# Attention scores in a ring of half banks, the softmax bias on VectorE, and other durations for the planner

## The chip, the cores and the metric

The kernel runs on one core of a Trainium2 chip. TensorE (PE) multiplies, VectorE (DVE) and ScalarE (ACT) work element by element and can read and write PSUM, GpSimd (POOL) works on SBUF, and SyncE (SP) issues most of the transfers. Each engine takes its instructions in the order in which they were written for it, and waits where an instruction names a semaphore that has not been reached. The metric is the device time of one launch in microseconds (us); the reference point is the median of three runs.

## The reference

Two independent halves are computed and put side by side in the output (2048 rows, 1024 + 1024 columns):

- A, attention over a sliding window: `qkv = x @ wqkv`, 32 heads of 32 columns, scores `q k^T / sqrt(32)` where `0 <= i - j < 256`, softmax, times `v`, then `@ wo`.
- B, a Fourier mixing layer by matrices: `a = x @ Wd_re^T`, `b = x @ Wd_im^T`, `y = Ws_re @ a - Ws_im @ b`.

All inputs and outputs are float32.

## The kernel before

Every large product is done on float16 pieces: a float32 operand is scaled and split into a high and a low float16 part, and three of the four part products are summed in PSUM (line 720). Blocks of such products are further combined by a scheme with seven instead of eight block products, whose sums and differences are made by POOL and DVE. A product tile is 128 partitions by 512 columns, one PSUM bank of 2 KB per partition, and it is filled by groups of matmuls; ACT and DVE then move it out.

Attention is done in 256 **blocks**: 8 groups of four heads, 16 tiles of 128 query rows, and two pairs of heads per group. The function `s_step` (line 562 on) records one block, for two heads j = 0, 1 at a time:

1. PE, line 586: scores of the query tile against its own and the previous key tile, 2 x 256 columns, into a tile `s`. For the tiles from the third on, a second product against the key tile two back, 2 x 128 columns, into a tile `old`. Together these are called score groups here: 256 into `s`, 224 into `old`.
2. DVE, line 597: a predicated copy that puts the entries of `old` that are inside the window over those of `s` that lie above the diagonal (or a constant where there is no `old`).
3. DVE, line 602: the negated maximum of each row, `mx`.
4. POOL, line 609: `bias = mx * scale + constant`, 128 x 2 values.
5. ACT, line 612: the exponential of each head's scores, in place in `s`, with that bias.
6. ACT, line 432, the high part, then DVE, line 436, the low part, both from `s` into the SBUF tile `hl`.
7. SP: a transposing transfer of `hl` into `t`; POOL, lines 627 and 630: masks on `t`; four blocks later PE, line 662: the product with `v` into the bank `pv`.

The eight PSUM banks are used thus: four for the products `m` (line 720), two for `s` (a ring of two tiles, each a whole bank for the two heads of a block), one for `old`, one for `pv`. `old` also takes the small transposes with which scale factors are found (lines 471 and 1058), read by DVE in lines 473 and 1060.

The order of all instructions is made by a list scheduler in the kernel's own Python (`Plan`). Every operation is recorded with an engine, an estimated duration, the buffers it reads and writes, and a ring: buffer k of a ring of n can be written when the last users of buffer k - n are done. PE operations get a due time from the sum of their durations, the others from what waits for them; each engine, when free, takes the ready operation that is due first. The operations are then issued in the order of their planned starts. What follows from that order is not the planner's: the framework that builds the program looks at the tiles that each instruction reads and writes, in that order, and adds the semaphore waits between engines. The planner knows only the buffers and keys that it was given.

Durations enter the plan as numbers: `c_act` for ACT, `c_mm` for matmuls, 0.26 for a small transpose, 0.034 for a matmul with `v`.

Of the kernel before, what the change touches and what calls it, by code (L numbers as in the profile page):

```python
# [10 lines left out]
F32 = mybir.dt.float32  # L11
# [6 lines left out]
ALU = mybir.AluOpType  # L18
AX = mybir.AxisListType

P = 128
# [28 lines left out]
BIAS = "POOL"  # L50
# [250 lines left out]
def c_act(n, ap=True):  # L301
    return 0.19 + 0.00084 * n + (0.09 if ap else 0.0)
# [26 lines left out]
def c_mm(n):  # L329
    return max(0.032, n / 2400.0 + 0.0025)  # L330
# [3 lines left out]
def fused_kernel(ctx: ExitStack, tc: tile.TileContext, xa, wqk, wv, wo, xb, wd, cs, out):  # L334
# [14 lines left out]
    ps_s = ctx.enter_context(tc.tile_pool(name="ps_s", bufs=2, space=PSUM))  # L349
# [17 lines left out]
    pshift = const.tile([P, 1], F32, name="pshift")  # L367
# [10 lines left out]
    def setup():  # L378
# [5 lines left out]
        nc.gpsimd.memset(pshift, PSHIFT)  # L384

    op("POOL", 1.0, setup, w=["ident", "upper", "never", "pshift"])
# [3 lines left out]
    old_ring = Ring(R, lambda k: ps_v.tile([P, CH], F32, tag="old", name=f"old_{k}"), 1, free=True)  # L390
    s_ring = Ring(R, lambda k: ps_s.tile([P, 2, 2 * P], F32, tag="s", name=f"s_{k}"), 2)
# [54 lines left out]
    def dve(cost, fn, r=(), w=(), port=False):  # L446
        op("DVE", cost, fn, r=r, w=w, port=port)
# [20 lines left out]
    def scale_of(key, v, s, wk, down=2.0 ** -14, loose=False):  # L468
        t1 = tops.pop(key)
        pt = old_ring.new()  # L470
        op("PE", 0.26, lambda: nc.tensor.transpose(pt.t[:, :P], t1.t[:, 0:1].to_broadcast([P, P]), ident),
# [8 lines left out]
        dve(0.53, rest, w=[wk])  # L480
# [48 lines left out]
    def attention():  # L529
# [33 lines left out]
        def s_step(b):  # L563
# [4 lines left out]
            S = s_ring.new()  # L568
# [3 lines left out]
            def scores(dst, k0, k_end, w):  # L572
                mats, cost, keys = [], 0.0, []
                for j in range(2):
                    h, k = 2 * hp + j, k0
                    while k < k_end:
# [4 lines left out]
                        cost += c_mm((k1 - k) * P) + 0.01  # L581
# [14 lines left out]
            sv = lambda: S.t[:, :, 2 * P - w:2 * P]  # L596
            dve(0.425, lambda: nc.vector.copy_predicated(  # L597
                S.t[:, :, P:2 * P], upper2,
                old.t[:, :2 * P].rearrange("p (j k) -> p j k", j=2) if nb == 3 else never2),
                r=["upper", "never"] + ([old] if nb == 3 else []), w=[(S, 0), (S, 1)])  # L600
            mx, bias = mx_ring.new(), bias_ring.new()
            dve(c_dve(2 * w), lambda: nc.vector.tensor_reduce(mx.t, sv(), axis=AX.X, op=ALU.max, negate=True),  # L602
                r=[(S, 0), (S, 1)], w=[mx])
            es = escs[:, g // 2, sc:sc + 1]
            if BIAS == "ACT":
                op("ACT", 0.387, lambda: nc.scalar.activation(bias.t, mx.t, AF.Identity, bias=pshift, scale=es),
                   r=[mx, "pshift", ("esc", g // 2)], w=[bias])
            else:
                op("POOL", 0.215, lambda: nc.gpsimd.tensor_scalar(bias.t, mx.t, es, PSHIFT, op0=ALU.mult, op1=ALU.add),  # L609
                   r=[mx, ("esc", g // 2)], w=[bias], port=True)  # L610
# [1084 lines left out]
```

## Time and profile before

| what | value |
|---|---|
| median of three runs | 1731.82 us (1731.67 to 1733.55) |
| profiled execution | 1732.34 us, its span 1730.6 us |
| PE busy | 1690.7 us (98% of the span), granted clock 1.00 |
| DVE busy | 1346.4 us (78%) |
| ACT busy | 1056.7 us (61%) |
| POOL busy | 776.7 us (45%) |

The span runs from the first to the last instruction, and the execution takes 1.7 us more than its span. Attention lies between the first score matmul at 262.4 us and the end of the last low part at 1504.1 us. A busy PE in these tables is PE with a matmul in flight. "Idle before" is time in which an engine had nothing running, with the instruction that ended it.

### The profile page before, as it was taken

How to read it: one execution, taken by the hardware profiler on the slowest of the kernel's cores; microseconds unless marked ns; L12 is line 12 of the kernel's file. 1: busy time of each engine (PE TensorE's matmuls, PEld its weight loads, DVE VectorE, ACT ScalarE, POOL GpSimd, SP SyncE). 2: the span in 40 equal slices, each digit the busy share in tenths (PEclk: the TensorE clock that was granted, in tenths of full speed). 3: DMA queues.
4: the chain of work that ended last, by engine and by line, in shares of the span. 5: the costliest groups of instructions: out<-in, count | busy, mean ns of one | idle time of the engine just before them, and what ended most of it. 6: DMA issues, size and time to landing. Idle time of an engine off the chain costs nothing.

```text
span 1730.6 us, 31866 instructions
## 1 busy us (share of the span) xinstructions
PE 1690.7 (98%) x11607; PEld 907.7 (52%) x11607; DVE 1346.4 (78%) x2294; ACT 1056.7 (61%) x1678; POOL 776.7 (45%) x979
## 2 busy tenths in 40 slices
PE   8999999999999999999999999999999999999998
PEld 3446787674545445545445555545555555544443
DVE  6978997677987888777798986789886688879641
ACT  7555635456767778777685756676665676553322
POOL 0133501314545646535765755676564666611000
PEclk9999999999999999999999999999999999999999
DMA  6389799999999779898499999769999658983331
GB/s 261 124 321 334 233 306 263 279 227 240 230 258 235 145 192 233 205 271 202 96 220 279 254 266 215 145 141 237 245 258 231 151 128 204 221 269 110 110 98 73
DMA packets 469918, 368.36 MB, mean 213 GB/s; under 512 B 341760, under 2 KB 412416, under 8 KB 469760
## 3 DMA queue, kind: packets, MB, share of 16 engines
q1 hardware_dynamic: 468896, 363.17, 81.0%
q0 software_dynamic: 864, 3.15, 1.2%
q8 instruction: 91, 1.49, 0.4%
q14 instruction: 67, 0.55, 0.1%
HBM read 195.97 MB, written 96.86 MB: 169 GB/s over the span
## 4 chain that ended last, share of the span: by engine, by line
PE 54%; DVE 15%; issue 8%; DMA 7%; ACT 7%; POOL 7%; SPq 1%; POOLq 0%; DVEq 0%; ACTq 0%
PE m L720 48%; PE pv L662 3%; POOL raw L1075 2%; DVE mx L602 2%; DVE st L1102 2%; ACT s L612 2%; POOL bias L609 2%; PE s L586 2%; DVE hl L436 2%; DMA t<-hl 1%; DVE s L597 1%; POOL t L630 1%; POOL z L627 1%; ACT hl L432 1%; DMA qk<-qs 1%
## 5 line engine op out<-in xcount | busy, mean ns | idle before, releaser
L720 PE MATMUL m<-reg,st 128*128 128x512 f16 x4776 | 1093.6, 379 | 13.6 <-DVE st L1102 3.6
L720 PEld LDWEIGHTS <-st 128*128 128x128 f16 x5400 | 512.5, 97 | 583.8 <-issue 15.1
L612 ACT ACTIVATE s<-s,bias,escs 128x256 f32<-128x256 f32 (+1 forms) x512 | 271.1, 530 | 286.2 <-POOL bias L609 277.4
L609 POOL TENSOR_SCALAR bias<-mx,escs 128x2 f32<-128x2 f32 x256 | 120.9, 472 | 400.5 <-DVE mx L602 308.6
L1075 POOL TENSOR_TENSOR raw<-raw,raw 128x512 f32<-128x512 f32 x128 | 175.8, 1374 | 186.6 <-DVE st L1102 174.7
L436 DVE TENSOR_TENSOR hl<-s,hl 128x512 f16<-128x512 f32 (+1 forms) x256 | 171.1, 669 | 96.5 <-ACT hl L432 95.7
L627 POOL TENSOR_SCALAR_AFFINE_SELECT z<-t 128x512 f16<-128x512 f16 x224 | 170.9, 766 | 60.0 <-DMA t<-hl 43.6
L630 POOL TENSOR_SCALAR_AFFINE_SELECT t<-t 128x512 f16<-128x512 f16 x224 | 170.5, 767 | 10.9
L602 DVE TENSOR_REDUCE mx<-s 128x2 f32<-128x512 f32 (+1 forms) x256 | 170.9, 668 | 4.8
L432 ACT ACTIVATE hl<-s 128x512 f16<-128x512 f32 (+1 forms) x256 | 148.0, 579 | 6.5 <-DMA t<-hl 3.1
L720 PEld LDWEIGHTS <-reg 128*128 128x128 f16 x1212 | 115.7, 98 | 63.2 <-issue 1.8
L1102 DVE SCALAR_TENSOR_TENSOR st<-raw,sc,st 128x1024 f16<-128x1024 f32 x96 | 134.1, 1400 | 16.5 <-ACT st L1101 16.2
L586 PEld LDWEIGHTS <-qk 96*128 96x128 f16 x1056 | 94.1, 97 | 85.8 <-issue 17.3
L1101 ACT ACTIVATE st<-raw,sc 128x1024 f16<-128x1024 f32 x96 | 109.6, 1146 | 34.5 <-PE m L720 14.5
L597 DVE COPY_PREDICATED s<-upper,old 128x256 f32<-128x256 uint32 x224 | 94.4, 421 | 29.3 <-PE old L586 21.8
L720 PE MATMUL m<-reg 128*128 128x512 f16 x480 | 114.7, 379 | 0.8 <-DVE reg L1512 0.5
L586 PE MATMUL s<-qk,qk 96*128 96x128 f16 (+1 forms) x608 | 96.0, 252 | 5.0 <-DVE hl L436 4.8
L720 PE MATMUL m<-xz,st 128*128 128x512 f16 x432 | 97.0, 379 | 3.4 <-ACT m L1193 3.4
L662 PE MATMUL pv<-vt,t 128*128 128x65 f16 x1984 | 98.4, 185 | 1.1 <-POOL t L630 1.0
L1512 DVE SCALAR_TENSOR_TENSOR ybig<-m,fu,ybig 128x512 f32<-128x512 f32 x112 | 83.4, 745 | 14.1 <-PE m L720 12.1
L662 PEld LDWEIGHTS <-t 128*128 128x128 f16 x1984 | 88.2, 96 | 9.8 <-POOL t L630 1.5
L662 PE MATMUL pv<-vt,z 128*128 128x65 f16 (+1 forms) x896 | 87.9, 185 | 4.2 <-DVE o L673 4.0
(172 smaller groups left out, 2124.7 us busy)
## 6 DMA issues: line engine op xcount, KB each, us to landing
raw<-in_cs_dram SPq DMA_DIRECT2D x64, 512.0 KB, 5.6
qk<-qs SPq DMA_DIRECT2D x192, 128.0 KB, 4.2
out_dram<-ybig SPq DMA_DIRECT2D x44, 512.0 KB, 5.4
qs<-ybig SPq DMA_DIRECT2D x64, 256.0 KB, 4.6
raw<-in_xb_dram SPq DMA_DIRECT2D x32, 512.0 KB, 5.4
raw<-in_wd_dram SPq DMA_DIRECT2D x32, 512.0 KB, 5.4
ybig<-out_dram SPq DMA_DIRECT2D x32, 512.0 KB, 5.3
vs<-ybig SPq DMA_DIRECT2D x32, 260.0 KB, 4.4
```

Of the source, the lines that this page charges most:

```text
L432: else nc.scalar.activation(dst(), src(), AF.Copy), r=r, w=w)
L436: op("DVE", c_dve(n), lambda: nc.vector.tensor_tensor(dst(), src(), hi(), op=ALU.subtract), r=r, w=w, port=port)
L586: nc.tensor.matmul(dst(j, a, e), qu.t[:, h, i * P:i * P + P], ku.t[:, h, ka:ke], start=True, stop=True, skip_group_check=True)
L602: dve(c_dve(2 * w), lambda: nc.vector.tensor_reduce(mx.t, sv(), axis=AX.X, op=ALU.max, negate=True), r=[(S, 0), (S, 1)], w=[mx])
L609: op("POOL", 0.215, lambda: nc.gpsimd.tensor_scalar(bias.t, mx.t, es, PSHIFT, op0=ALU.mult, op1=ALU.add), r=[mx, ("esc", g // 2)], w=[bias ...
L612: op("ACT", 0.32 + 0.00085 * w, lambda h=h: nc.scalar.activation(sv()[:, h], sv()[:, h], AF.Exp, bias=bias.t[:, h:h + 1], scale=es), r=[bi ...
L627: op("POOL", 0.637, lambda: nc.gpsimd.affine_select(out=z.t, in_=pk(), compare_op=ALU.is_gt, fill=0.0, base=0, pattern=[[0, 4], [-1, P]], ...
L630: op("POOL", 0.637, lambda: nc.gpsimd.affine_select(out=pk(), in_=pk(), compare_op=ALU.is_ge, fill=0.0, base=0, pattern=[[0, 4], [1, P]], ...
L662: nc.tensor.matmul(pvt()[:, r, j, lo:], lhs, vt.t[:, k % QB, at + lo:at + VW], start=a, stop=e, skip_group_check=True)
L720: nc.tensor.matmul(ps.t[:, j * n:j * n + n], lhs(), rhs(), start=first, stop=last, skip_group_check=True)
L1075: lambda: e.tensor_tensor(o(), a(), b(), op=ALU.subtract if sub else ALU.add), r=r, w=w, port=True)
L1102: op("DVE", c_dve(n, True), lambda: nc.vector.scalar_tensor_tensor(dst(1), src(), scl(), dst(0), op0=ALU.mult, op1=ALU.subtract), r=[*r, s ...
```

## The change

- The two tiles `s` and the tile `old` become one tile `sall` of six half banks (256 float32 columns each), three banks in all. A block takes two half banks, one for each head, from a ring of five; `old` is the sixth, alone in its own ring of one. The halves of a block are, block after block, (0, 1), (2, 3), (4, 0), (1, 2), (3, 4), and again. Two halves share a bank: 0 with 1, 2 with 3, 4 with `old`. An access to both heads is a view of `sall` with the step between its two halves.
- The bias is computed by DVE instead of POOL, with `C_TINY` (0.155) as its planned duration; the constant `pshift` goes.
- Durations in the plan: `c_act` 0.142 + 0.00089 n (+ 0.083) instead of 0.19 + 0.00084 n (+ 0.09), small transposes 0.12 instead of 0.26, a score matmul without its extra 0.01, a matmul with `v` 0.0265 or 0.0297 instead of 0.034, the scale arithmetic after a transpose 0.47 instead of 0.53.

What each instruction computes stays; the number of matmuls, copies, reductions and exponentials stays too.

```diff
 def c_act(n, ap=True):
-    return 0.19 + 0.00084 * n + (0.09 if ap else 0.0)
+    return 0.142 + 0.00089 * n + (0.083 if ap else 0.0)
...
-    ps_s = ctx.enter_context(tc.tile_pool(name="ps_s", bufs=2, space=PSUM))
+    ps_s = ctx.enter_context(tc.tile_pool(name="ps_s", bufs=1, space=PSUM))
...
-    old_ring = Ring(R, lambda k: ps_v.tile([P, CH], F32, tag="old", name=f"old_{k}"), 1, free=True)
-    s_ring = Ring(R, lambda k: ps_s.tile([P, 2, 2 * P], F32, tag="s", name=f"s_{k}"), 2)
+    sall = ps_s.tile([P, 6, 2 * P], F32, name="sall")
+    old_ring = Ring(R, lambda k: sall[:, 5], 1, free=True)
+    s_ring = Ring(R, lambda k: sall[:, k % 5], 5)
...
-        op("PE", 0.26, lambda: nc.tensor.transpose(pt.t[:, :P], t1.t[:, 0:1].to_broadcast([P, P]), ident),
+        op("PE", 0.12, lambda: nc.tensor.transpose(pt.t[:, :P], t1.t[:, 0:1].to_broadcast([P, P]), ident),
...
-            S = s_ring.new()
+            s0, s1 = sorted((s_ring.new() for _ in range(2)), key=lambda b: b.k % 5)
+            both = lambda: sall[:, s0.k % 5:s1.k % 5 + 1:s1.k % 5 - s0.k % 5]
...
-                        cost += c_mm((k1 - k) * P) + 0.01
+                        cost += c_mm((k1 - k) * P)
...
-            scores(lambda j, a, e: S.t[:, j, (2 - n2 + a) * P:(2 - n2 + e) * P], qb + 1 - n2, qb + 1, [(S, 0), (S, 1)])
+            scores(lambda j, a, e: (s0, s1)[j].t[:, (2 - n2 + a) * P:(2 - n2 + e) * P], qb + 1 - n2, qb + 1, [s0, s1])
...
             dve(0.425, lambda: nc.vector.copy_predicated(
-                S.t[:, :, P:2 * P], upper2,
-                old.t[:, :2 * P].rearrange("p (j k) -> p j k", j=2) if nb == 3 else never2),
-                r=["upper", "never"] + ([old] if nb == 3 else []), w=[(S, 0), (S, 1)])
+                both()[:, :, P:2 * P], upper2,
+                old.t.rearrange("p (j k) -> p j k", j=2) if nb == 3 else never2),
+                r=["upper", "never"] + ([old] if nb == 3 else []), w=[s0, s1])
...
-            if BIAS == "ACT":
-                op("ACT", 0.387, lambda: nc.scalar.activation(bias.t, mx.t, AF.Identity, bias=pshift, scale=es),
-                   r=[mx, "pshift", ("esc", g // 2)], w=[bias])
-            else:
-                op("POOL", 0.215, lambda: nc.gpsimd.tensor_scalar(bias.t, mx.t, es, PSHIFT, op0=ALU.mult, op1=ALU.add),
-                   r=[mx, ("esc", g // 2)], w=[bias], port=True)
+            dve(C_TINY, lambda: nc.vector.tensor_scalar(bias.t, mx.t, es, PSHIFT, op0=ALU.mult, op1=ALU.add),
+                r=[mx, ("esc", g // 2)], w=[bias])
             for h in range(2):
                 op("ACT", 0.32 + 0.00085 * w, lambda h=h: nc.scalar.activation(
                     sv()[:, h], sv()[:, h], AF.Exp, bias=bias.t[:, h:h + 1], scale=es),
-                   r=[bias, ("esc", g // 2)], w=[(S, h)])
+                   r=[bias, ("esc", g // 2)], w=[(s0, s1)[h]])
...
-            hi_op(hi, sv, None, 2 * w, [(S, 0), (S, 1)], [(hl, 0)], False)
-            lo_op(lo, sv, None, hi, 2 * w, [(S, 0), (S, 1), (hl, 0)], [(hl, 1)], False)
+            hi_op(hi, sv, None, 2 * w, [s0, s1], [(hl, 0)], False)
+            lo_op(lo, sv, None, hi, 2 * w, [s0, s1, (hl, 0)], [(hl, 1)], False)
...
-                        cost += 0.034
+                        cost += 0.0265 if part else 0.0297
```

The changed kernel is five lines shorter, so that its lines stand lower: the scores are line 585 there, the predicated copy 596, the maximum 601, the bias 604, the exponential 607, the high part 430, the low part 434, the products 715.

**On DVE**, in the middle of attention (block 77 and the one after it), this is the order before, with the semaphores that each instruction waits for. `DVE_`, `PE_`, `Activation_` and `Pool_` are the engines, `DMAHW` is a transfer.

```order
L597 COPY_PREDICATED s_7472<-upper,old_7583 128x2x128 [waits PE_49]
L1102 SCALAR_TENSOR_TENSOR reg_81<-raw_7239,sc_7543,reg_81 128x512 [waits DMAHW0_49,Activation_49]
L602 TENSOR_REDUCE mx_7606<-s_7472 128x2 [waits DVE_49]
L597 COPY_PREDICATED s_7594<-upper,old_7599 128x2x128 [waits PE_49]
L667 RECIPROCAL rs_7618<-pv_7554 128x4
L602 TENSOR_REDUCE mx_7621<-s_7594 128x2 [waits DVE_49]
L669 TENSOR_REDUCE pv_7554<-pv_7554 128x128 [waits DVE_49]
L673 TENSOR_TENSOR o_7405<-pv_7554,rs_7618 128x2x64 [waits DVE_49]
L1102 SCALAR_TENSOR_TENSOR st_7635<-raw_7249,sc_7543,st_7635 128x1024 [waits DMAHW1_49,Activation_49]
L436 TENSOR_TENSOR hl_7656<-s_7472,hl_7656 128x512 [waits DMAHW4_49,Activation_49]
```

The same blocks in the changed kernel:

```order
L596 COPY_PREDICATED sall<-upper,sall 128x2x128 [waits Activation_49]
L601 TENSOR_REDUCE mx_7420<-sall 128x2 [waits Activation_49]
L434 TENSOR_TENSOR hl_7405<-sall,hl_7405 128x512 [waits DMAHW7_49,PE_49]
L604 TENSOR_SCALAR bias_7444<-mx_7420,escs 128x2 [waits DVE_49]
L1097 SCALAR_TENSOR_TENSOR reg_81<-raw_7123,sc_7386,reg_81 128x512 [waits DMAHW1_49,Activation_49]
L596 COPY_PREDICATED sall<-upper,sall 128x2x128 [waits DVE_49,Activation_49]
L662 RECIPROCAL rs_7462<-pv_7407 128x4
L601 TENSOR_REDUCE mx_7464<-sall 128x2 [waits DVE_49]
L664 TENSOR_REDUCE pv_7407<-pv_7407 128x128 [waits DVE_49]
L604 TENSOR_SCALAR bias_7475<-mx_7464,escs 128x2 [waits DVE_49]
L668 TENSOR_TENSOR o_7239<-pv_7407,rs_7462 128x2x64 [waits DVE_49]
L434 TENSOR_TENSOR hl_7471<-sall,hl_7471 128x512 [waits DMAHW0_49,Activation_49]
```

The bias stands behind the maximum of its block, with one instruction or none between. The copy waits for ACT, a maximum waits for ACT although it reads what the copy before it wrote, and a low part waits for PE.

**On PE**, the two score groups of a block (line 586) stood together before, each behind a wait for DVE:

```order
L586 LDWEIGHTS qk_7_5744
L586 MATMUL s_6361<-qk_7_5597,qk_7_5744 128x256 [waits DVE_49]
L586 LDWEIGHTS qk_7_5744
L586 MATMUL s_6361<-qk_7_5597,qk_7_5744 128x256
L586 LDWEIGHTS qk_7_5744
L586 MATMUL old_6365<-qk_7_5597,qk_7_5744 128x128 [waits DVE_49]
L586 LDWEIGHTS qk_7_5744
L586 MATMUL old_6365<-qk_7_5597,qk_7_5744 128x128
```

The two groups of the same block in the changed kernel; the one into `old` (128 columns) stands first, the other 20 rows later, with matmuls of line 715 between:

```order
L585 LDWEIGHTS qk_7_5667
L585 MATMUL sall<-qk_7_5410,qk_7_5667 128x128 [waits Activation_49]
L585 LDWEIGHTS qk_7_5667
L585 MATMUL sall<-qk_7_5410,qk_7_5667 128x128
L715 LDWEIGHTS st_5696
```

```order
L585 LDWEIGHTS qk_7_5667
L585 MATMUL sall<-qk_7_5410,qk_7_5667 128x256 [waits Activation_49]
L585 LDWEIGHTS qk_7_5667
L585 MATMUL sall<-qk_7_5410,qk_7_5667 128x256
L715 LDWEIGHTS st_5696
```

The groups have come apart and changed places, and both wait for ACT now, although ACT never touches the half bank of `old`. Over the whole program the rows of line 586 (585) that wait for ACT go from 16 to 190 and those that wait for DVE from 398 to 179; the maxima that wait for PE or ACT go from 0 to 107, the copies that wait for ACT from 0 to 97, the low parts that wait for PE from 0 to 81, the high parts that wait for PE or DVE from 0 to 143.

More of the change, by code (lines that the diff above doesn't have):

```diff
@@ L49 @@
 TBUF = 6
-BIAS = "POOL"
 SUMS = ("POOL", "POOL", "POOL", "POOL")
@@ L383, in setup @@
         nc.gpsimd.memset(never, NEG)
-        nc.gpsimd.memset(pshift, PSHIFT)
-    op("POOL", 1.0, setup, w=["ident", "upper", "never", "pshift"])
+    op("POOL", 1.0, setup, w=["ident", "upper", "never"])
     a_ring, b_ring, c_ring = (Ring(R, lambda k, t=t, n=n: ps_m.tile([P, CH], F32, tag=f"m{t + k % n}", name=f"m{t + k % n}_{k}"), n)
                               for t, n in ((0, 2), (2, 1), (3, 1)))
-    old_ring = Ring(R, lambda k: ps_v.tile([P, CH], F32, tag="old", name=f"old_{k}"), 1, free=True)
-    s_ring = Ring(R, lambda k: ps_s.tile([P, 2, 2 * P], F32, tag="s", name=f"s_{k}"), 2)
+    sall = ps_s.tile([P, 6, 2 * P], F32, name="sall")
+    old_ring = Ring(R, lambda k: sall[:, 5], 1, free=True)
+    s_ring = Ring(R, lambda k: sall[:, k % 5], 5)
     pv_ring = Ring(R, lambda k: ps_v.tile([P, CH], F32, tag="pv", name=f"pv_{k}"), 1, free=True)
@@ L478, in rest @@
             nc.vector.reciprocal(s, v)
[L480 removed]
+        dve(0.47, rest, w=[wk])
     vx = const.tile([P, 2, 2], F32, name="vx")
```

7 lines of the change are left out of this document (3 added, 4 removed).

## The prediction

> **What bounds the kernel now.** I read the page's head first.
>
> ```profile
> span 1730.6 us, 31866 instructions
> PE 1690.7 (98%) x11607; PEld 907.7 (52%) x11607; DVE 1346.4 (78%) x2294; ACT 1056.7 (61%) x1678; POOL 776.7 (45%) x979
> PEclk9999999999999999999999999999999999999999
> ```
>
> PE has work in flight for 98% of the span at full granted clock, so the kernel is PE's queue and 1730.6 - 1690.7 = 39.9 us besides. No edit here takes a matmul away: whatever is gained comes out of these 39.9 us, and whatever makes PE wait is added in full. Next, the busy time by stage, cut where attention begins and ends (columns: stage, its length, busy time and instructions of PE, PEld, DVE, ACT, POOL, granted clock, DMA share, GB/s).
>
> ```profile
> 0.00:262.40 262.40, 253.57 (x1529) 153.01 (x1529) 219.20 (x284) 149.44 (x197) 62.48 (x69) 1.00 0.75 262
> 262.40:1504.10 1241.70, 1219.86 (x9052) 656.48 (x9052) 994.32 (x1860) 833.66 (x1392) 694.14 (x894) 1.00 0.91 216
> 1504.10:1730.60 226.50, 217.28 (x1033) 98.20 (x1029) 132.87 (x151) 73.58 (x89) 20.09 (x16) 1.00 0.45 136
> ```
>
> The change lives in the middle stage of 1241.7 us, 4.85 us for each of the 256 blocks, in which PE is idle for 21.8 us, DVE for 247.4 and ACT for 408.0. Who keeps PE waiting there:
>
> ```profile
> PE s L586 <- DVE hl L436: 4.8, 8, 1.3
> PE pv L662 <- DVE o L673: 4.0, 6, 1.4
> PE m L720 <- DVE st L1102: 3.4, 4, 1.0
> PE old L586 <- DVE sc L1060: 2.4, 4, 1.1
> PE old L586 <- DVE s L597: 2.2, 1, 2.2
> ...
> PE pv L662 <- POOL t L630: 0.3, 1, 0.3
> ```
>
> The first five make 16.8 us, all waits of PE in the stage 20.7 (us, times, longest). That is the whole prize. Only the first and the last, 7.0 us, hang on the chain from scores to low part that the change shortens.
>
> **The ring.** A block takes buffers 2p and 2p+1 of five, so it needs 2p-5 and 2p-4 back; 2p-4 is a buffer of block p-2. Both buffers of a block have the low part as their last user, since it reads both heads. So the scores of block p wait for the low part of block p-2, as with two whole banks. The planner gets no freedom from the fifth half bank: gain 0, and no reason for another value.
>
> **The one tile.** `sall` replaces three tiles (two `s` in turn, and `old`). In the order of the changed kernel the maxima, copies, low and high parts now wait for engines with whose work on their own block they had finished. I followed every access to `sall` through the built program's waits: each one is held back until the accesses issued ahead of it by the other engines are done, also where halves and banks differ, wherever one of the two writes. Of the 480 score groups, about nine in ten now wait for an access that doesn't touch the half they write. The planner doesn't know these waits and plans the accesses on top of each other, as they ran before. How often they did:
>
> ```profile
> 262.40:1504.10 1241.70, 96.04 (x608) 438.67 (x768) 415.88 (x768) 1.00 0.91 216
> ...
> 262.40:1504.10 1241.70, 71.77 (x485) 5.00 (x37) 104.76 (x261) 1.00 0.91 216
> ```
>
> ```profile
> L612 ACT ACTIVATE s<-s,bias,escs 128x256 f32<-128x256 f32 (+1 forms) x512 | 271.1, 530 | 286.2 <-POOL bias L609 277.4
> L436 DVE TENSOR_TENSOR hl<-s,hl 128x512 f16<-128x512 f32 (+1 forms) x256 | 171.1, 669 | 96.5 <-ACT hl L432 95.7
> L602 DVE TENSOR_REDUCE mx<-s 128x2 f32<-128x512 f32 (+1 forms) x256 | 170.9, 668 | 4.8
> L432 ACT ACTIVATE hl<-s 128x512 f16<-128x512 f32 (+1 forms) x256 | 148.0, 579 | 6.5 <-DMA t<-hl 3.1
> L597 DVE COPY_PREDICATED s<-upper,old 128x256 f32<-128x256 uint32 x224 | 94.4, 421 | 29.3 <-PE old L586 21.8 <-PE s L586 6.7
> ```
>
> The first fence is the stage once more, for the instructions on `s` alone (PE, DVE, ACT) and on `old` alone (PE, PEld, DVE). DVE works on score banks for 438.67 + (104.76 - 94.4, the copy being in both) = 449 us, 36% of the stage, and ACT for 415.88, 33.5%. If the two are independent, 0.36 + 0.335 - 0.12 = 57.5% of the stage has one of them at a score tile. PE arrives 256 + 224 + 37 = 517 times (score groups, and the 37 small transposes into `old`). That is 297 arrivals on top of another access. The accesses are 0.42 to 0.67 us long, weighted by their time 0.58, so 0.29 us are left on average: 297 x 0.29 = 86 us. What a change of hands costs stands in one block:
>
> ```profile
> 1007.71 0.69 DVE L602 TENSOR_REDUCE mx<-s 128x2 f32<-128x512 f32 x1
> ...
> 1008.50 0.27 POOL L609 TENSOR_SCALAR bias<-mx,escs 128x2 f32<-128x2 f32 x1 [3.68 <-DVE mx L602]
> 1008.80 1.11 ACT L612 ACTIVATE s<-s,bias,escs 128x256 f32<-128x256 f32 x2 [3.36 <-POOL bias L609]
> ...
> 1013.82 0.59 ACT L432 ACTIVATE hl<-s 128x512 f16<-128x512 f32 x1
> 1014.44 0.69 DVE L436 TENSOR_TENSOR hl<-s,hl 128x512 f16<-128x512 f32 x1 [1.16 <-ACT hl L432]
> 1015.19 0.38 PE L586 MATMUL s<-qk,qk 96*128 96x256 f16 x2
> ```
>
> ACT to DVE 0.03 us (1014.41 to 1014.44), DVE to PE 0.06 (1015.13 to 1015.19). With 0.05 the term is 297 x 0.34 = 101 us. I also counted it in the timeline of the stage: of 517 PE accesses, from the first row to the last low part below, 287 start while DVE or ACT is at a score tile, and what is then left of that access adds up to 93.7 us.
>
> ```profile
> 262.44 0.49 PE L586 MATMUL s<-qk,qk 96*128 96x128 f16 x4
> ...
> 1503.36 0.69 DVE L436 TENSOR_TENSOR hl<-s,hl 128x512 f16<-128x512 f32 x1
> ```
>
> I take **+94 us**, between the two. PE's queue is in order, so the products of line 720 behind a waiting score group stand too, and with them the engines that empty their banks. Below: PE falls back behind the others, so that more of the foreign access is over when it comes; half of the term, 47. Above: 101.
>
> **DVE and ACT at the same gate.** By the same count, 246 of ACT's accesses and 167 of DVE's start on top of another's, with 65.2 and 45.3 us left (high against low part, both only reading, not counted): 110 us of waits in engines with 408 and 247 us of idle time. Behind a waiting copy or maximum on DVE stand the evictions of line 1512, for which the products wait, and the low part, for which the scores of the next block but one wait. That wait has little room in part of the blocks: of 254 low parts, 49 were followed by the next score group within 0.3 us, as at 1015.13 above. So about a fifth reaches PE: **+22 us**; none is the lower end, all 110 the upper.
>
> **The bias.** POOL loses 256 instructions and DVE gets them. The nearest row of DVE is a scalar operation on one column:
>
> ```profile
> L609 POOL TENSOR_SCALAR bias<-mx,escs 128x2 f32<-128x2 f32 x256 | 120.9, 472 | 400.5 <-DVE mx L602 308.6 <-DVE rs L667 55.5 <-DVE topone L464 14.7
> L1067 DVE TENSOR_SCALAR fu<-fa,sc 128x1 f32<-128x1 f32 x31 | 6.0, 195 | 0.0
> ```
>
> 256 x 0.2 = 51 us on DVE, under its 247 us of idle time; without that cover it would be 51 on the path. The way from maximum to exponential, 0.40 us in the block shown (1008.40 to 1008.80), loses a change of hands. That can give back at most the 7.0 us above: **-5**. POOL's 121 us lie beside the path, since PE waited for POOL's masks 0.3 us in the stage.
>
> **The planned durations** change no instruction, only places in queues. At best they remove what is left of the 20.7 us, at worst they add as much, since neither row says which: 0.
>
> Sum: 1730.6 + 94 + 22 - 5 = 1841.6 us of span. The profiled execution took 1732.34, 1.7 over its span, and the median 1731.82 is 1.2 over it; with 1.2 the time is **1843 us**. From the ends: 1730.6 + 47 - 20.7 + 1.2 = 1758 and 1730.6 + 101 + 110 + 20.7 + 1.2 = 1964. The likeliest case itself lies within 1790 to 1900.
>
> **Rivals.**
>
> *The score tile itself becomes the bound.* One access at a time: 449 + 416 + 168 (PE, 96.04 + 71.77) = 1033 us. The changed order hands the tile from engine to engine 1421 times; at 0.045 us that is 64, together 1097 of 1241.7 us, 88%, for a resource on which three busy engines must meet in a fixed order. If all that overlapped (94 + 110) and all handing over lands on the end: 1731.8 + 204 + 64 = 2000. For it: the 88%. Against it: four fifths of the low parts end with room before the next scores. It decides once DVE and ACT are regularly behind when PE has arrived.
>
> *PE's falling back takes most of it.* The access that PE waits for is fixed by the order, so after a few waits it may be over in time. A third of 94 and little else: 1731.8 + 31 + 6 - 5 = 1764. Against it: that access often hangs on scores which PE itself delivered late.
>
> *Only halves of one bank exclude each other.* Consecutive blocks share a bank in two of five steps, and `old` shares one with half 4, used by two blocks of five: 0.4 x (94 + 22) - 5 = 41, thus 1773. The rows of the order speak against it. The Trainium skill, "PSUM — Partial Sum Buffer", section "PSUM bank collisions raise a hardware error", asks for no more than this: engines are to be kept apart by bank (and quadrant of partitions), and different banks may be used at once. The accesses of the trace before, in separate banks, did run at once.
>
> *Faster.* The foreign accesses are over when PE comes, and the shorter chain and the better durations work: between -7.0 and -20.7, so 1711 to 1725. It needs PE to find the tile free in nearly all of 517 arrivals, where 287 were not free before.
>
> **How the numbers follow.** Forecast 50%, the tile as the bound 18% (most of it 1900 to 2000, little above), falling back 12%, banks only 8%, faster 7%, no change 3%; 2% lie elsewhere on the slow side. The range 1750 to 1960 holds the forecast, the two small slow cases and half of the tile's. Two measurements of this kernel can be told apart from about 0.2%. Faster by more than that 7%, within it 3%, slower 90%.
>
> **What would show it.** Right: PE busy again near 1691 us (plus the drain at each new stop), and new idle time before the score groups, waits of 0.1 to 0.6 us in some 250 to 400 places, put down to the exponential, the maximum and the high and low parts, together 70 to 130 us; PE's other waits up by some 20; stages before 262 and after 1504 as long as before. The bias row on DVE near 0.2 us, POOL down by 120 us. Wrong in size: score waits under 40 us (falling back, or banks only), or a DVE and ACT with long waits on score tiles and PE idle for over 200 us (the tile as the bound). Wrong altogether: PE's waits for score tiles still under 15 us, which would mean that the waits in the order are met before PE comes.

## The result, and the profile after

The changed kernel took 1960.19 us (median; 1958.05 to 1963.38), the kernel before beside it 1731.67 (1730.02 to 1733.55): a ratio of 1.1328, 95% interval 1.1315 to 1.1342. The forecast was 1843, so the direction was right and the loss of 228.5 us is about twice the 111 forecast. 1960.19 lies just outside the range.

The head of the page after (busy time and share of the span), and the span by stage (columns as in the prediction), cut where attention now begins and ends:

```profile
span 1961.7 us, 31930 instructions
PE 1747.4 (89%) x11607; PEld 911.3 (46%) x11607; DVE 1426.4 (73%) x2550; ACT 1069.0 (54%) x1678; POOL 639.2 (33%) x722
```

```profile
0.00:262.50 262.50, 253.55 (x1529) 152.96 (x1530) 220.78 (x284) 149.03 (x197) 62.98 (x68) 1.00 0.75 262
262.50:1743.40 1480.90, 1283.89 (x9072) 663.16 (x9070) 1075.35 (x2114) 847.31 (x1393) 555.35 (x637) 0.99 0.76 182
1743.40:1961.70 218.30, 209.95 (x1011) 95.19 (x1008) 130.24 (x154) 72.61 (x88) 20.92 (x18) 1.00 0.45 135
```

Nothing happened before attention; attention takes 239.2 us longer (1480.9 against 1241.7), the end 8.2 us less. In attention PE is idle for 197.0 us instead of 21.8. Next, what PE waited for (us, times, longest) over the whole span:

```profile
PE sall L585 <- ACT sall L607: 63.6, 81, 2.3
PE sall L585 <- DVE hl L434: 38.0, 43, 2.2
PE sall L585 <- ACT hl L430: 30.4, 38, 2.0
PE sall L585 <- DVE mx L601: 28.2, 31, 1.9
PE sall L1053 <- ACT sall L607: 8.6, 7, 1.5
PE sall L1053 <- DVE mx L601: 6.4, 7, 1.9
```

All waits of PE for the tile together are 188.7 us in 230 places, where `s` and `old` cost 9.4 in 13. Its other waits fell from 25.4 to 19.2 us. (A wait is idle time of more than 0.15 us.) That closes the account of the span: 231.1 = 179.3 of waits for the tile - 6.2 of others + 1.3 of idle time put down to nothing + 56.7 of longer busy time. Of the 56.7 about 17 go with the granted clock of 0.990 instead of 1.000 (1747.4 x 0.01); the other 39 go with the stops. PE waits 257 times where it waited 51 times before, which is 0.19 us for each stop more. The other five kernels with a shared tile (part 2 below) give 0.16 to 0.19 us in the same way: busy time multiplied by the granted clock, less the same for the kernel before, divided by the waits added. This is an estimate from the traces, in which the ends of matmuls are modelled.

The groups that use the tile (busy time, mean ns of one | idle time of their engine before them and what ended it):

```profile
L607 ACT ACTIVATE sall<-sall,bias,escs 128x256 f32<-128x256 f32 (+1 forms) x512 | 271.3, 530 | 387.5 <-DVE bias L604 181.0 <-PE sall L585 55.1 <-DVE sall L596 40.9
L434 DVE TENSOR_TENSOR hl<-sall,hl 128x512 f16<-128x512 f32 (+1 forms) x256 | 171.5, 671 | 116.6 <-ACT hl L430 65.4 <-ACT sall L607 26.1 <-PE sall L585 15.9
L601 DVE TENSOR_REDUCE mx<-sall 128x2 f32<-128x512 f32 (+1 forms) x256 | 171.5, 671 | 55.9 <-ACT hl L430 24.3 <-PE sall L585 15.4 <-ACT sall L607 12.4
L430 ACT ACTIVATE hl<-sall 128x512 f16<-128x512 f32 (+1 forms) x256 | 148.4, 581 | 85.9 <-DVE mx L601 23.3 <-PE sall L585 17.6 <-DVE sall L596 15.0
L596 DVE COPY_PREDICATED sall<-upper,sall 128x256 f32<-128x256 uint32 x224 | 95.6, 427 | 106.8 <-PE sall L585 55.3 <-ACT sall L607 25.1 <-ACT hl L430 18.4
L604 DVE TENSOR_SCALAR bias<-mx,escs 128x2 f32<-128x2 f32 x256 | 92.4, 361 | 1.7
```

The means are those of before, so no access became slower; they wait. The maxima had 4.8 us of idle time ahead of them in all and now have 55.9, of which 24.3 are behind the high part of some other block; the high parts had 6.5 and have 85.9; the copies 29.3 and 106.8. By a count over all instructions from 262.5 to 1743.4, one engine alone is in the tile for 1032 us, two at once never, and none for 449; before, two or three engines at once were in `s` and `old` for 159 us of the 1241.7.

How such a wait is built stands in one piece of the timeline (start, duration; in brackets the idle time before, and what ended it):

```profile
792.14 2.11 PE L715 MATMUL m<-reg,st 128*128 128x512 f16 x9
792.55 0.60 ACT L430 ACTIVATE hl<-sall 128x512 f16<-128x512 f32 x1 [0.76 <-DVE mx L601]
793.18 0.69 DVE L434 TENSOR_TENSOR hl<-sall,hl 128x512 f16<-128x512 f32 x1 [0.24 <-ACT hl L430]
793.91 1.11 ACT L607 ACTIVATE sall<-sall,bias,escs 128x256 f32<-128x256 f32 x2 [0.76 <-DVE hl L434]
794.94 0.68 ACT L1504 ACTIVATE ybig<-m,fu 128x512 f32<-128x512 f32 x1
795.51 0.60 ACT L430 ACTIVATE hl<-sall 128x512 f16<-128x512 f32 x1
796.16 0.27 PE L585 MATMUL sall<-qk,qk 96*128 96x128 f16 x2 [1.91 <-ACT hl L430]
796.53 0.69 DVE L434 TENSOR_TENSOR hl<-sall,hl 128x512 f16<-128x512 f32 x1 [1.99 <-PE sall L585]
```

PE runs dry at 794.25 and is due to write two halves of the tile. The access whose turn it is ahead of PE is the high part of 795.51. It had not begun, since ACT did its exponentials (themselves held until the low part of 793.18 had ended) and then an eviction that has nothing to do with scores. PE stands for 1.91 us for an instruction of 0.60. Behind PE stands the low part of that block: its high part has ended at 796.11, and it starts at 796.53, after the scores. The order of turns is fixed when the program is built, so nobody can step in where another is late.

### The profile page after: what moved, and what is told of

It is laid out like the page before. It is cut to its first block, busy times and chain, and to the rows that moved or that the text cites. A ratio compares the mean times of both kernels' runs of the same rounds, so it can differ in the third digit from the quotient of the medians.

```text
span 1961.7 us, 31930 instructions
## 1 busy us (share of the span) xinstructions
PE 1747.4 (89%) x11607; PEld 911.3 (46%) x11607; DVE 1426.4 (73%) x2550; ACT 1069.0 (54%) x1678; POOL 639.2 (33%) x722
## 5 line engine op out<-in xcount | busy, mean ns | idle before, releaser
L715 PE MATMUL m<-reg,st 128*128 128x512 f16 x4776 | 1118.0, 383 | 11.7 <-DVE st L1097 4.8
L607 ACT ACTIVATE sall<-sall,bias,escs 128x256 f32<-128x256 f32 (+1 forms) x512 | 271.3, 530 | 387.5 <-DVE bias L604 181.0
L622 POOL TENSOR_SCALAR_AFFINE_SELECT z<-t 128x512 f16<-128x512 f16 x224 | 160.0, 717 | 464.3 <-DMA t<-hl 334.9
L585 PE MATMUL sall<-qk,qk 96*128 96x128 f16 (+1 forms) x1056 | 141.6, 238 | 170.9 <-ACT sall L607 63.6
L434 DVE TENSOR_TENSOR hl<-sall,hl 128x512 f16<-128x512 f32 (+1 forms) x256 | 171.5, 671 | 116.6 <-ACT hl L430 65.4
L601 DVE TENSOR_REDUCE mx<-sall 128x2 f32<-128x512 f32 (+1 forms) x256 | 171.5, 671 | 55.9 <-ACT hl L430 24.3
L430 ACT ACTIVATE hl<-sall 128x512 f16<-128x512 f32 (+1 forms) x256 | 148.4, 581 | 85.9 <-DVE mx L601 23.3
L596 DVE COPY_PREDICATED sall<-upper,sall 128x256 f32<-128x256 uint32 x224 | 95.6, 427 | 106.8 <-PE sall L585 55.3
L1096 ACT ACTIVATE st<-raw,sc 128x1024 f16<-128x1024 f32 x96 | 109.5, 1142 | 42.0 <-PE m L715 30.2
L604 DVE TENSOR_SCALAR bias<-mx,escs 128x2 f32<-128x2 f32 x256 | 92.4, 361 | 1.7
L996 ACT ACTIVATE junk<-raw 128x1024 uint8<-128x1024 f32 x82 | 86.1, 1050 | 8.2 <-DMA raw<-in_cs_dram 7.6
```

The lines of the kernel that those rows point to most:

```text
L430: else nc.scalar.activation(dst(), src(), AF.Copy), r=r, w=w)
L434: op("DVE", c_dve(n), lambda: nc.vector.tensor_tensor(dst(), src(), hi(), op=ALU.subtract), r=r, w=w, port=port)
L585: nc.tensor.matmul(dst(j, a, e), qu.t[:, h, i * P:i * P + P], ku.t[:, h, ka:ke], start=True, stop=True, skip_group_check=True)
L607: op("ACT", 0.32 + 0.00085 * w, lambda h=h: nc.scalar.activation(sv()[:, h], sv()[:, h], AF.Exp, bias=bias.t[:, h:h + 1], scale=es), r=[bi ...
L622: op("POOL", 0.637, lambda: nc.gpsimd.affine_select(out=z.t, in_=pk(), compare_op=ALU.is_gt, fill=0.0, base=0, pattern=[[0, 4], [-1, P]], ...
L715: nc.tensor.matmul(ps.t[:, j * n:j * n + n], lhs(), rhs(), start=first, stop=last, skip_group_check=True)
```

## The experiments

All ratios are against the kernel before, with the 95% interval, run beside it on the same chip.

**1. Which part of the change costs.** Four kernels, each with a part of it. In the first, `s` and `old` stay three tiles, and the bias and the durations are as changed; in the second the kernel before gets only one tile, with each block in a bank of its own:

```diff
...
+    sall = ps_s.tile([P, 6, 2 * P], F32, name="sall")
-    old_ring = Ring(R, lambda k: ps_v.tile([P, CH], F32, tag="old", name=f"old_{k}"), 1, free=True)
-    s_ring = Ring(R, lambda k: ps_s.tile([P, 2, 2 * P], F32, tag="s", name=f"s_{k}"), 2)
+    old_ring = Ring(R, lambda k: sall[:, 4:6].rearrange("p j k -> p (j k)"), 1, free=True)
+    s_ring = Ring(R, lambda k: sall[:, k % 2 * 2:k % 2 * 2 + 2], 2)
```

The third moves only the bias, the fourth changes only the planned durations, each as in the change.

> The change with the one tile taken back: two whole-bank tiles for the scores and a tile of its own for the old block, as before, but the bias on VectorE and the new durations stay. Theory (the one tile makes every access wait for the last one of the other engines): the whole loss goes, 1715 to 1740 us, waits of PE for score tiles under 15 us. Rival (the bias on VectorE, 256 instructions that measured 361 ns each, holds up the queue of VectorE): half or more of the loss stays, above 1840 us.

> The kernel before with one edit: the two score tiles and the old tile become one tile of three banks, each block still in a whole bank of its own and the old block in the third, the bias on POOL, the old durations. Theory (the tile, not the bank, is what is held apart): most of the loss comes, 1900 to 2000 us, with waits of PE for the tile of 150 us or more. Rival (only halves in one bank exclude each other): no two blocks share a bank here, so 1725 to 1745 us.

> The kernel before with the bias on VectorE and nothing else. Theory: 51 to 92 us more work on VectorE under its 247 us of idle time, chain from maximum to exponential shorter: 1722 to 1738 us. Rival (VectorE's queue is the hidden bound): 1750 us or more.

> The kernel before with the new planned durations and nothing else. Theory: places in queues change, no more: 1720 to 1743 us. Rival (the durations make the planner bring blocks so close that PE runs into them): 1760 us or more.

| kernel | us | ratio |
|---|---|---|
| three tiles, bias and durations | 1748.14 | 1.0103 [1.0084, 1.0123] |
| one tile of three banks, nothing else | 1925.33 | 1.1127 [1.1109, 1.1144] |
| bias on VectorE alone | 1740.74 | 1.0061 [1.0046, 1.0076] |
| durations alone | 1733.05 | 1.0022 [1.0009, 1.0034] |

The one tile costs 196 us by itself, with each block's scores and the old block in whole banks of their own. PE's waits in it:

```profile
PE sall L587 <- DVE hl L437: 44.6, 50, 2.1
PE sall L587 <- ACT sall L613: 41.3, 59, 1.9
PE sall L587 <- ACT hl L433: 40.8, 50, 1.9
PE sall L587 <- DVE mx L603: 15.2, 20, 1.4
```

So what is held apart is the tile, not the bank, and the rival of the banks is out. The three tiles and the bias missed what was expected of them: without the one tile a loss of 1.0% is left, 0.6% of it already with the bias alone. Part 3 is on that.

**2. Why one tile costs so much.** The ring and the tile without bias and durations; the changed kernel whose planner is told of the exclusion; the kernel before with only its two score banks in one tile; the changed kernel with its exponentials written elsewhere. The telling, in the list scheduler's loop and at the two rings; `o.excl` marks an operation on a buffer of a shared ring, `tile` holds until when the tile is planned as used and by which engine:

```diff
...
+            if o.excl:
+                tile[0], tile[1] = max(tile[0], fin), e
...
+                if o.excl and e != tile[1] and tile[0] > t + 1e-9:
+                    skipped.append(item)
+                    put(tile[0], "free", o)
...
+    s_ring.shared = old_ring.shared = True
...
```

The exponentials aside:

```diff
...
+    ex_ring = att_ring("ex", [P, 2, 2 * P], F32, 2)
...
-                    sv()[:, h], sv()[:, h], AF.Exp, bias=bias.t[:, h:h + 1], scale=es),
+                    ev()[:, h], sv()[:, h], AF.Exp, bias=bias.t[:, h:h + 1], scale=es),
...
```

> The ring and the one tile alone: bias on GpSimd and the planner's durations as in the kernel before. Theory (one tile held apart as a whole costs nearly all, the ring earns nothing because block p must still wait for the low part of block p-2): bias and durations together cost 1.0% with three tiles, so this stands some 15 to 20 us under the changed kernel's 1960, at 1930 to 1950, and not under the 1925 of one tile in which every block had its own bank. Rival (the ring's third place earns something that the one tile hides): under 1915.

> The changed kernel, whose list scheduler is also told that two engines may not be in the score tile at once: a row on another engine that would start while the tile is in use is put off until it is free, and the scheduler takes other work of that engine ahead of it. Theory (the loss is waits that the order was not made for: PE stands 189 us at the tile in 230 waits, while projection matmuls are at hand): PE's waits for the tile fall under half, time 1780 to 1870. Rival (the tile itself is full, and no order helps: 1053 us of accesses and their hand-overs in a chain that the blocks must go through): 1920 to 1980, and the waits stay over 150 us.

> The kernel before, with its two score banks made one tile of two banks, and the old blocks in a tile of their own as before: half the amount of what the run with three banks in one tile (1925 us) joined. PE then comes to the shared tile once a block in place of twice (256 times in place of 480). Theory (PE pays by the arrival at a gate whose foreign accesses stand in line themselves): the loss against the kernel before is about half to two thirds of that run's 196 us, so 1830 to 1870. Rival (the chain of VectorE's and ScalarE's accesses is the bound, which the old blocks hardly touch: 967 of 1053 us remain): over 1890. Second rival (what is lost is only PE's direct wait at a running access, a mean 0.33 us as I predicted): under 1790.

> The changed kernel with one thing taken out of the score tile: the exponentials are written to a buffer of their own in SBUF, and the high and low parts are read from there, so that 512 of the 1421 accesses and 320 of the 1053 us leave the tile (five buffers of turned weights in place of six and three of masked ones in place of four make room). Theory (the time in which the tile is used by others sets PE's waits, which grow faster than in proportion, since who holds the tile was held itself): the 68 us that PE waits for high and low parts go, and some of the rest, 1810 to 1880. Rival (VectorE's and ScalarE's own work is what limits, 1426 and 1069 us busy): over 1920. Second rival (the waits go in full with the room in the tile): under 1790.

The last of them needed a control, the same with the kernel before's three tiles:

> The control for the run with the exponentials aside: the kernel before with three tiles as they were, the exponentials written to a buffer of their own in SBUF and the parts read from there, with five turned and three masked buffers. It also sets a score bank free two accesses earlier. Theory (PE hardly waits for a score bank: 5.0 us ahead of its 608 score matmuls; and the low part, 831 ns from SBUF in that run against 671 from PSUM, adds some 40 us to VectorE, which has room): no gain, 1728 to 1760, so that the part of the 98 us which the buffer took off the changed kernel is owed to the tile alone. Rival (the earlier free bank lets scores run ahead and PE idles less): 1705 to 1722.

| kernel | us | ratio | PE's waits for the shared tile |
|---|---|---|---|
| as changed | 1960.19 | 1.1328 [1.1315, 1.1342] | 188.7 us in 230 |
| ring and one tile alone | 1931.71 | 1.1175 [1.1156, 1.1193] | 169.5 in 213 |
| one tile, own banks | 1925.33 | 1.1127 [1.1109, 1.1144] | 170.1 in 220 |
| two score banks in one tile | 1879.22 | 1.0862 [1.0844, 1.0880] | 130.3 in 148 |
| as changed, exponentials aside | 1862.24 | 1.0773 [1.0754, 1.0791] | 108.5 in 140 |
| as changed, planner told | 1854.60 | 1.0720 [1.0704, 1.0736] | 72.6 in 95 |
| before, exponentials aside | 1767.47 | 1.0210 [1.0189, 1.0230] | none shared |

The mean wait is 0.76 to 0.88 us in the six kernels with a shared tile. In five of them the loss is 0.9 to 1.0 us for each wait at the tile; where the planner was told it is 1.3, with 39.4 us of other waits and the lowest granted clock. The ring earns nothing: half banks took 0.5% more than whole ones in the same single tile, a difference for which another order may be enough.

The planner alone, with every tile, bank and instruction as changed, takes back 106 of the 228 us. Its largest waits of PE:

```profile
PE sall L594 <- DVE hl L443: 16.1, 22, 1.5
PE sall L594 <- DVE sall L605: 12.5, 12, 3.7
PE sall L594 <- ACT sall L616: 12.5, 11, 4.4
PE m L724 <- DVE st L1106: 11.2, 17, 1.7
PE m L724 <- ACT m L1197: 10.5, 12, 2.0
```

The tile was therefore not full: a better order of the same accesses needs less time. But 125 us stay, part of them as new waits for other things (the last two rows), part as busy time: its granted clock was 0.984, and 1735.5 us of busy PE at that clock are some 28 more than at full clock. What a perfect order would leave of them was not tried.

With the old blocks in a tile of their own PE comes 256 times instead of 480, and 149 of 196 us stay. That is more than the half to two thirds expected and less than the rival's figure, so the number of arrivals is not the measure. That VectorE's and ScalarE's accesses hold each other up without PE, and that this reaches PE, fits it but was not taken apart. Taking the high and low parts out of the tile brings 98 us, although the buffer, with the smaller rings that make room for it, has a price, which the control shows as 37 us, more than either of the control's expectations allowed. If that price is the same in both, the tile's share is 135 us of the 228, for 31% of the time in which it is used (320 of 1032 us; the 1421 in the expectation is the number of changes of hands, not of accesses).

**3. The bias.** With three tiles, on VectorE, under two more planned durations (0.37 and 0.26 us instead of 0.155), and with the mark that the planner has for operations in which VectorE and GpSimd exclude each other. Beside these, for the worth of a new order alone, GpSimd's own bias planned at 0.47 instead of 0.215; and the bias on ScalarE, in the form that the kernel before already had, with the old durations and with the new ones. The mark, against the third kernel of part 1, and the bias on ScalarE, against the kernel before:

```diff
-            dve(C_TINY, lambda: nc.vector.tensor_scalar(bias.t, mx.t, es, PSHIFT, op0=ALU.mult, op1=ALU.add),
-                r=[mx, ("esc", g // 2)], w=[bias])
+            dve(0.22, lambda: nc.vector.tensor_scalar(bias.t, mx.t, es, PSHIFT, op0=ALU.mult, op1=ALU.add),
+                r=[mx, ("esc", g // 2)], w=[bias], port=True)
```

```diff
-BIAS = "POOL"
+BIAS = "ACT"
```

> Only the bias moved to VectorE, as in the run that cost 0.6%, but the planner is given 0.37 us for it, which that run's trace shows (376 ns), in place of 0.155. Theory A (256 rows planned 0.22 us too short, 56 us in all, make VectorE late against the plan, and PE's order is made for the plan): back to within 0.2% of the kernel before, 1727 to 1733. Theory B (96 us more on VectorE, which becomes 84% busy in the stage of attention, stand ahead of what PE waits for, whatever is planned): stays 0.4 to 0.8% slower, 1736 to 1744.

> How much the order alone moves the time: the kernel before, with the same instructions on the same engines, where the planner is given 0.47 us for the bias on GpSimd, as the trace shows it (472 ns), in place of 0.215. Theory (a new draw of the list scheduler's order costs some tenths of a per cent by itself, up or down, as the run with the traced durations did with 0.2%): within 0.4% of the kernel before, 1724 to 1738. Rival (honest numbers for the bias send rows the wrong way, by whatever engine has it: with 0.37 told for VectorE the time went from +0.6% to +1.1%): 1738 to 1750.

> Only the bias moved to VectorE, as in the two runs that cost 0.6% and 1.1%, with the planner given 0.26 us for it, between their 0.155 and 0.37. Theory (the move itself costs, whatever order is drawn): 1738 to 1752 again. Rival (those two were unlucky draws of the order): within 0.3% of the kernel before, 1725 to 1735.

> Only the bias moved to VectorE, planned at 0.22 us (its median row was 228 ns), and marked for the planner like the other operations that VectorE and GpSimd can't do at the same time: the planned end is put off while such an operation of the other engine runs. Theory A (the price is the unplanned exclusion: a third of the bias rows stand until GpSimd's instruction is over): the plan allows for it, 1728 to 1738, at most +0.4%. Theory B (the exclusion is real, but the planner only lengthens the operation and still puts it there, so PE's waits for VectorE stay): 1738 to 1760, as with the other three plans, with bias rows over 350 ns in the mean. Theory C (no exclusion): mean and time as in the other three.

> Only the bias moved, to ScalarE in place of VectorE (the form for it was in the kernel before; planned 0.387 us): some 256 x 0.39 = 100 us of work on an engine with 408 us of idle time in the stage. Theory (a bias whose engine GpSimd can't stop costs little): rows of one length, longest not over twice the median, and a time within 0.4% of the kernel before, 1724 to 1738. Rival (any engine on the path from maximum to exponential pays for it, and taking it from GpSimd is what costs): over 1740.

> The bias on ScalarE together with the changed kernel's planned durations (which alone cost 0.2%): another order, the same place for the bias. Theory (the place of the bias earns the 1.0%: maximum to exponential needs one change of engines in place of two, nothing of it meets GpSimd, and ScalarE has the room): 0.6 to 1.2% faster than before, 1711 to 1721. Rival (the run with the bias on ScalarE was a lucky draw of the order): within 0.4% of before, 1724 to 1738.

| bias on, planned at | us | ratio | bias row, mean ns |
|---|---|---|---|
| VectorE, 0.155 (part 1) | 1740.74 | 1.0061 [1.0046, 1.0076] | 376 |
| VectorE, 0.37 | 1750.39 | 1.0107 [1.0091, 1.0123] | 387 |
| VectorE, 0.26 | 1757.16 | 1.0159 [1.0138, 1.0181] | 375 |
| VectorE, 0.22 and the mark | 1741.39 | 1.0060 [1.0038, 1.0083] | 395 |
| GpSimd, 0.47 | 1727.58 | 0.9986 [0.9976, 0.9995] | 464 |
| ScalarE, 0.387 | 1714.65 | 0.9902 [0.9886, 0.9919] | 384 |
| ScalarE, 0.387, new durations | 1716.45 | 0.9926 [0.9909, 0.9942] | 384 |

Three of these missed what was expected of them: 0.37 and 0.26 us on VectorE lost more than any of their cases, and ScalarE, first tried, gained where nothing or a loss was expected. Two new orders with the bias left on GpSimd moved the time by 0.1 and 0.2%, one down and one up. The first three kernels on VectorE differ from each other in the order alone, by up to 1.0%, so the size of one such loss says little. The signs are alike: all four on VectorE lose 0.6 to 1.6%, both on ScalarE gain 0.7 and 1.0%. That points to the place of the bias, as far as four and two orders can. The bias rows of the first kernel of the table, and then of the one on ScalarE (minimum/median/longest ns, first and last start in us):

```profile
L605 DVE TENSOR_SCALAR bias<-mx,escs x256: 192/228/1980, 263.4 to 1505.5; 128x2 f32<-128x2 f32 x128
```

```profile
L606 ACT ACTIVATE bias<-mx,pshift,escs x256: 372/387/393, 263.5 to 1479.6; 128x2 f32<-128x2 f32 x128
```

On ScalarE all are alike; on VectorE some are nine times as long as the median. One of these, in the same kernel on VectorE:

```profile
442.01 1.27 POOL L1071 TENSOR_TENSOR raw<-raw,raw 128x512 f32<-128x512 f32 x1 [17.93 <-DVE mx L602]
442.04 1.27 DVE L605 TENSOR_SCALAR bias<-mx,escs 128x2 f32<-128x2 f32 x1
443.22 0.74 DVE L1098 SCALAR_TENSOR_TENSOR reg<-raw,scw,reg 128x512 f16<-128x512 f32 x1
443.34 0.43 ACT L608 ACTIVATE s<-s,bias,escs 128x128 f32<-128x128 f32 x1 [0.24 <-DVE bias L605]
```

A bias of two columns ends with GpSimd's addition of 512 columns, 1.27 us later. In that kernel 85 of the 256 bias rows are over 0.3 us, 58.0 us together, and GpSimd is busy during 57.0 of them; during the 38.2 us of the 171 shorter rows it is busy for 7.0. The Trainium skill, "SBUF — State Buffer", section "SBUF: two separate sides", says that VectorE and GpSimd share a pair of SBUF ports as an exclusive lock, which a VectorE instruction in a two-port mode, or with two SBUF inputs against a GpSimd instruction that reads SBUF, has to take, and that the loser stands for the whole instruction of the other. The rows agree in the length of the stand; which of the two conditions the bias meets, no run shows. The mark did not keep the two apart: in that kernel 86 bias rows are over 0.3 us, 62.8 us together, with GpSimd busy during 61.6. What the bias on VectorE would cost without the overlap was therefore not seen.

On ScalarE maximum and exponential are one change of engines apart, not two, and what PE waited for fell (us, times, longest):

```profile
PE m L720 <- ACT m L1193: 4.0, 3, 1.9
PE s L586 <- DVE hl L436: 2.6, 5, 1.1
PE m L720 <- DVE st L1102: 1.8, 5, 0.8
```

All waits for VectorE: 14.5 us against 26.0 before, 30.2 to 37.4 in the first three kernels of the table, and 27.3 in the fourth. The bias rows take 98.4 us of ScalarE, which had 408 us of idle time. The kernel before with the bias on ScalarE is 1.0% faster than the kernel before, and 12.5% faster than the changed one by the two medians (1714.65 of 1960.19). Neither the shorter way nor GpSimd's 121 us set free is enough for a gain: the bias on VectorE, which also made the maximum, has both and loses. What VectorE's place has beside them is the rows under GpSimd and a fuller engine (busy for 81% of the span, ScalarE with the bias for 66%). These two were not tried apart, so the cause of the 0.6 to 1.6% is argued, not shown.

## Why the prediction was right and wrong

**The step that failed is the term of one tile, +94 us**, taken from 287 arrivals of PE on top of a running access with 0.33 us of it left. After the change 230 waits were seen, a little under that count, but with a mean of 0.82 us. I sorted them by the tile's last access by VectorE or ScalarE ahead of each. In 89 waits it was running when PE stopped, 36.1 us in all, 0.41 each. That is the kind that I counted, and it is under half of the term. In the other 141 it had not begun, 152.5 us, 1.08 each: it began 0.44 us after PE had stopped, on average. In 80 of these the access came after idle time of its own engine, so it was held itself, at the tile or by what it reads; in 61 it came straight behind other work of that engine. I counted collisions in the old timeline and moved only the one who arrives; in the new order every delay makes the next access late, and PE has to wait for a given access rather than for the tile to be free. The planner told of the exclusion, with 72.6 us of such waits and 106 us less time, shows that about half of the loss comes from the order made without them. One more thing stood in the sum at nothing: the signs name a drain at each new stop, but no term holds it, and PE's busy time rose by 56.7 us, some 39 of them with the stops.

**VectorE and ScalarE at the gate, 110 us of which a fifth reaches PE, +22.** The idle time ahead of the five kinds of access rose from 432.5 to 770.4 us (sums of their rows, the copies without old blocks included), by 338 us, three times the count. How much of it reaches PE cannot be taken apart from the first term in the changed kernel, but the two score banks in one tile, where PE's arrivals are nearly halved and three quarters of the loss remain, speak for much more than a fifth.

**The ring, 0:** right, or a little under it (0.5% in the same single tile). **The durations, 0:** right in size, 0.2% slower alone.

**The bias, -5:** wrong in sign; alone it cost 0.6%, some 11 us by the interval's middle. I took 0.2 us from a row of 31 instructions of one column, and the mean was 361 ns in the changed kernel. The median, 228, is near it; nearly all of the difference is in 76 rows over 0.3 us, 52.0 us together, with GpSimd busy during 50.9. I also reckoned VectorE's idle time as cover for all of it, but the bias stands between maximum and exponential, where a late row holds up what follows.

**The rivals.** Halves of one bank: out by the one tile with own banks. Falling back: out; PE's lateness did not make the foreign accesses early, because they were late too. Faster: out. The tile as the bound came nearest in size, "most of it 1900 to 2000", and one part of its mechanism is what was seen, foreign accesses late when PE comes; but the tile is free for 449 of 1481 us, and a better order helps, so a full resource was not the reason.

**The signs that I named.** Waits of 0.1 to 0.6 us in 250 to 400 places, together 70 to 130: the number was nearly right, length and sum were not. PE's other waits up by some 20 us: they fell by 6. PE busy near 1691 us plus drains: 1747.4. The stages before 262 and after 1504 as before: yes for the first; the end is 8 us shorter, since some of its work had moved into the longer attention. POOL down by 120: by 137.5. Bias row near 0.2 us: 361 ns.

What the prediction cites from the Trainium skill, "PSUM — Partial Sum Buffer", section "PSUM bank collisions raise a hardware error", is not contradicted by the 196 us of separate banks in one tile: those waits stand in the program that the framework builds.

## What to carry to other kernels

Buffers that several engines use at the same time should be tiles of their own: what the framework orders by is the tile, whatever parts and banks the views name, and the scheduler knows nothing of it. When a new exclusion is priced from an old timeline, the remainder of running accesses is only a lower bound; the access that one waits for can itself be late, and here waits for accesses that had not begun made 152.5 of 188.6 us. Each wait also has a price beside its length, here 0.16 to 0.19 us of PE's busy time by estimate. The place of a small operation is not settled by its length alone: the same two columns cost 0.6 to 1.6% on VectorE and earned 0.7 to 1.0% on ScalarE, where every row is longer than VectorE's median.

## What was not expected of the hardware

VectorE's low part, reading the exponentials from SBUF instead of PSUM, took 857 ns in the mean (control of part 2) against 669, with a median of 692 against 684. The kernel before, and then the control (minimum/median/longest ns):

```profile
L436 DVE TENSOR_TENSOR hl<-s,hl x256: 409/684/693, 266.1 to 1503.4; 128x512 f16<-128x512 f32 x112, 128x256 f16<-128x256 f32 x16
```

```profile
L436 DVE TENSOR_TENSOR hl<-ex,hl x256: 410/692/2549, 266.7 to 1536.1; 128x512 f16<-128x512 f32 x115, 128x256 f16<-128x256 f32 x13
```

From SBUF 101 of the 256 rows are over 0.75 us, 115.6 us together, and GpSimd was busy during 103.9 of them. From PSUM no row is longer than 0.693 us, although GpSimd was busy during 93.7 of their 171.3 us. So here the exponentials in PSUM kept VectorE's low part out of GpSimd's way.

The granted clock was 0.984 to 0.996 in the profiles of the kernels with a shared tile, 0.996 to 1.000 in the others. It does not simply follow the number of PE's waits (0.984 with 155 waits, 0.996 with 243), and why it is lower was not tried. A difference of 1% is some 17 us of busy PE here.
